# The last batch's MLP by seven quarter products in place of eight, in a fused attention and mixer kernel

## The chip, the cores and the metric

The kernel runs on one core of one Trainium2 chip. The metric is the device time of one execution in microseconds (us), the median of the runs shown. Engines are named as the profile names them: PE (matrix product), PEld (its weight load), DVE (vector), ACT (activation), POOL (GpSimd), SP (a queue that here issues DMAs).

## The reference

Block-sparse attention over 4 batches, 8 heads, 768 positions and head width 64, then a mixer: a low-rank mix over the positions, and an MLP with one hidden layer of 2048, added to its own input.

```
mask = (neighbouring blocks) | (first or last block) | (three sampled blocks per row of blocks)
attn = softmax(where(mask, q @ k.T / sqrt(64), -1e9))
x    = (attn @ v), heads side by side          # (4, 768, 512)
h    = x.transpose(0, 2, 1) @ U @ V            # rank 32, over the 768 positions
u    = x + h.transpose(0, 2, 1)
out  = u + maximum(u @ w_ch1, 0) @ w_ch2       # 512 -> 2048 -> 512
```

## The kernel before

The work is done by head pairs, i = 0 to 15, four for each batch. Scores are made transposed (keys on the partitions), ACT takes their exponentials into slots of the tile est, and for i >= 4 the DVE multiplies them by the 0/1 tile mask, 1536 columns at a time (L756, two operands in SBUF). The value product (L400) takes the masked slot as the stationary operand. The DVE divides by the row sums into xh (16 bit) and xf (32 bit), the mix is added to both (L541, L542), and a transposing DMA from SP makes uT, the MLP's input with channels on the partitions.

The MLP of a batch has two layers. In w1 (L587) a unit is one block jj of 128 hidden channels and one half c of 384 positions: 4 products of 384 columns are summed in one PSUM bank, and ACT or DVE writes the positive part to a tile tT (L599, L601). In w2 (L611) a unit is a block sc of 128 positions: 16 products of 512 columns, four at a time (words W), then the DVE adds xf (L619) into a tile of, and SP sends it out. The last block of the last batch is done by last_half (L636, L644), 256 columns and then twice 128, so that its results leave in pieces; its tiles of come from a pool of two buffers.

The order on PE, DVE, ACT and SP is written by hand: the string PLAN holds one word for each piece of work, in the order in which it is issued (U: a w1 unit, W: four w2 products, a and b: the positive part on ACT or DVE, Q: scores of a pair, e: exponentials, p: mask product, V: value product, v: division, D and d: the mix, f: finish). A digit after a capital is the PSUM bank of the eight. The instructions of each engine then run in that order, and each waits for its operands. POOL is not in that list: its order is the compiler's. It casts the loaded q, k and v to 16 bit (L137, L140), issues the loads of the weights w1t and w2t, and has nothing to do in the batch-3 MLP. The casts from pair 6 on are cut into four pieces:

```
    for h in range(2):
        for ts in (slice(0, T // 2), slice(T // 2, T)):
            last = nc.gpsimd.tensor_copy(out=dst[:, h, ts], in_=ld[:, h, ts])
```

begin(i) is called when the first score of pair i comes up in PLAN, and loads(i) asks for the q, k and v of pair i + 2.

## Time and profile before

| what | value |
|---|---|
| median of 3 runs | 285.96 us (283.65 to 286.66) |
| profiled execution, from its first to its last instruction | 281.5 us |
| PE busy | 273.6 us, 97% of the span |
| DVE busy | 194.2 us, 69% |
| ACT busy | 177.9 us, 63% |
| POOL busy | 75.6 us, 27% |
| granted PE clock, mean | 0.999 |

No other time is given for the profiled execution than its span: what lies around it, the start and end of the program, is the difference to the timed runs, 2.1 to 5.2 us. A busy PE is an engine with a matmul in flight, and matmuls overlap, so 97% says that it seldom runs dry and not that it is at its peak. Rows of groups give the busy time of the group, the mean of one instruction in ns and the idle time just before, with what ended it.

### The profile page before, as it was taken

The numbers are of one execution on the slowest core, as the hardware profiler recorded it, in microseconds if no ns is written. First come the engines' busy times: TensorE is split into PE (matmuls) and PEld (weight loads), VectorE is DVE, ScalarE is ACT, GpSimd is POOL, SyncE is SP. The second block draws the span as 40 slices with busy tenths as digits, with TensorE's granted clock in tenths as the row PEclk, the third lists the DMA queues.
The fourth block names the chain that finished last, engine by engine and source line by source line (L and its number), as shares of the span: only waits on it lengthen the run. The fifth ranks groups of instructions, "written<-read, shape, count | busy, mean of one in ns | idle before, by whom it ended". The sixth has DMA issues, their size and how long they took to land.

```text
span 281.5 us, 6704 instructions
## 1 busy us (share of the span) xinstructions
PE 273.6 (97%) x2768; PEld 159.8 (57%) x2768; DVE 194.2 (69%) x347; ACT 177.9 (63%) x206; POOL 75.6 (27%) x164
## 2 busy tenths in 40 slices
PE   7899999999999999999999999999999999999993
PEld 3577775656465654656455654656547645555552
DVE  5699988988676898788677888776677871003411
ACT  3999998888668655686867555797776303451100
POOL 5379015901768050074352050060000000000000
PEclk9999999999999999999999999999999999999999
DMA  6799997999975653646351843740001062002021
GB/s 170 236 317 270 196 245 182 178 106 266 212 178 188 191 162 98 178 115 196 87 178 40 249 106 95 204 113 7 37 37 40 17 135 77 0 0 77 0 93 57
DMA packets 49118, 37.53 MB, mean 133 GB/s; under 512 B 30464, under 2 KB 45600, under 8 KB 49088
## 3 DMA queue, kind: packets, MB, share of 16 engines
q1 hardware_dynamic: 45968, 32.61, 42.9%
q0 software_dynamic: 2688, 4.19, 10.5%
q8 instruction: 21, 0.34, 0.5%
q10 hardware_dynamic: 432, 0.31, 0.4%
q14 instruction: 9, 0.07, 0.1%
HBM read 27.67 MB, written 6.29 MB: 121 GB/s over the span
## 4 chain that ended last, share of the span: by engine, by line
PE 92%; DVE 4%; DMA 2%; issue 1%; ACT 1%; SPq 0%; DVEq 0%; ACTq 0%
PE ps L587 30%; PE ps L611 29%; PE ps L400 12%; PE ps L741 10%; PE ps L697 3%; PE ps L716 2%; PE ps L529 2%; DMA qld<-in_q_dram 1%; PE ps L656 1%; DMA out_dram<-of 1%; DVE qres L686 1%; PE ps L636 1%; PE ps L670 1%; DVE kres L279 1%; ACT est L724 1%
## 5 line engine op out<-in xcount | busy, mean ns | idle before, releaser
L750 ACT ACTIVATE est<-ps 128x1536 f16<-128x1536 f32 x72 | 100.3, 1449 | 38.7 <-PE ps L741 38.7
L587 PE MATMUL ps<-uT,w1t 128*128 128x384 f16 x512 | 94.3, 326 | 0.0
L611 PE MATMUL ps<-w2t,tT 128*128 128x512 f16 x368 | 87.1, 379 | 0.0
L756 DVE TENSOR_TENSOR est<-est,mask 128x1536 f16<-128x1536 f16 x72 | 69.6, 972 | 15.2 <-ACT est L750 15.0
L599 ACT ACTIVATE tT<-ps 128x384 f16<-128x384 f32 x90 | 43.0, 494 | 43.5 <-PE ps L587 42.3
L587 PEld LDWEIGHTS <-w1t 128*128 128x128 f16 x512 | 47.6, 98 | 36.3 <-issue 5.8
L611 PEld LDWEIGHTS <-tT 128*128 128x128 f16 x368 | 34.4, 98 | 39.7 <-issue 3.8
L400 PEld LDWEIGHTS <-est 128*128 128x128 f16 x1152 | 40.8, 97 | 7.0 <-issue 1.9
L400 PE MATMUL ps<-vt,est 128*128 128x65 f16 x1152 | 43.4, 193 | 0.0
L140 POOL CAST stqld<-qld 128x192 f16<-128x192 f32 x40 | 16.9, 464 | 83.0 <-DMA qld<-in_q_dram 59.3
L619 DVE TENSOR_TENSOR of<-xf,ps 128x512 f32<-128x512 f32 x23 | 15.7, 683 | 27.6 <-PE ps L611 25.5
L601 DVE TENSOR_SCALAR tT<-ps 128x384 f16<-128x384 f32 x38 | 21.1, 555 | 18.8 <-PE ps L587 18.0
L741 PE MATMUL ps<-qpl,kpl 64*128 64x512 f16 (+1 forms) x288 | 31.3, 325 | 0.0
L706 ACT ACTIVATE est<-ps 128x768 f16<-128x768 f32 x30 | 22.5, 813 | 0.6 <-PE ps L697 0.6
L741 PEld LDWEIGHTS <-kpl 64*128 64x128 f16 x288 | 11.8, 94 | 15.9 <-issue 10.4
L140 POOL CAST stkld<-kld 128x192 f16<-128x192 f32 x40 | 18.7, 506 | 2.6 <-DMA kld<-in_k_dram 2.6
L477 DVE TENSOR_TENSOR xh<-ps,rcp 128x384 f16<-128x384 f32 x32 | 17.8, 557 | 1.1
L477 DVE TENSOR_TENSOR xf<-ps,rcp 128x384 f32<-128x384 f32 x32 | 17.5, 547 | 0.0
L541 DVE TENSOR_TENSOR xh<-xh,ps 128x384 f16<-128x384 f16 x28 | 15.3, 548 | 1.7 <-PE ps L529 1.6
L140 POOL CAST vt<-vld 128x192 f16<-128x192 f32 x40 | 15.9, 436 | 0.3 <-DMA vld<-in_v_dram 0.3
L542 DVE TENSOR_TENSOR xf<-xf,ps 128x384 f32<-128x384 f32 x28 | 15.3, 546 | 0.0
L697 PE MATMUL ps<-qres,kres 128*128 128x384 f16 x60 | 14.0, 324 | 0.8 <-DVE kres L279 0.5
(83 smaller groups left out, 149.5 us busy)
## 6 DMA issues: line engine op xcount, KB each, us to landing
vld<-in_v_dram SPq DMA_DIRECT2D x16, 384.0 KB, 5.0
out_dram<-of SPq DMA_DIRECT2D x23, 256.0 KB, 2.1
qld<-in_q_dram SPq DMA_DIRECT2D x15, 384.0 KB, 6.8
kld<-in_k_dram SPq DMA_DIRECT2D x15, 384.0 KB, 4.5
w1t<-in_moe_w_ch_dram POOLq DMA_DIRECT2D x4, 512.0 KB, 9.2
w2t<-in_moe_w_ch_dram POOLq DMA_DIRECT2D x4, 512.0 KB, 10.4
qld<-in_q_dram SPq DMA_DIRECT2D x2, 192.0 KB
uT<-xh SPq DMA_TRANSPOSE x14, 2.8
```

Of the source, the lines that this page charges most:

```text
L140: last = nc.gpsimd.tensor_copy(out=dst[:, h, ts], in_=ld[:, h, ts])
L400: nc.tensor.matmul(pav[:, sc, :], est[:, n, sc * P : (sc + 1) * P], vts[b % 2][:, 2 * hp + h, g, 0 : D + 1], start=(g == 0 and sc == 0), s ...
L477: nc.vector.tensor_tensor(out=dst, in0=pav[:, :, 0:D], in1=rcp[:, :, None].broadcast_to([P, T, D]), op=ALU.mult,)
L587: nc.tensor.matmul(pt, w1t[:, cc, jj * P : (jj + 1) * P], bts[b].uT[cc][:, c * HS : (c + 1) * HS], start=(cc == 0), stop=(cc == NCC - 1), ...
L599: nc.scalar.activation(out=dst, in_=pt, func=AF.Relu)
L601: nc.vector.tensor_scalar_max(out=dst, in0=pt, scalar1=0.0)
L611: nc.tensor.matmul(po, tts[b, c, jj][:, s * P : (s + 1) * P], w2t[:, jj, :], start=(jj == 0), stop=(jj == NJJ - 1),)
L697: nc.tensor.matmul(ps[:, c], kT[:, h, g * P : (g + 1) * P], qT[:, h, c * HS : (c + 1) * HS], start=True, stop=True,)
L706: lambda: nc.scalar.activation(out=dst, in_=ps, func=AF.Exp, scale=0.125),
L741: nc.tensor.matmul(units[h][:, u * S + lo : u * S + hi], kT[drows[h], g * P : (g + 1) * P], qT[drows[h], lo:hi], start=True, stop=True, sk ...
L750: nc.scalar.activation(out=both[h], in_=units[h].rearrange("p (g n) -> p g n", g=2), func=AF.Exp, scale=0.125,)
L756: lambda: nc.vector.tensor_mul(out=both[h], in0=both[h], in1=mask[:, 2 * j : 2 * j + 2, :]),
```

## The change

Only the last batch's MLP changes. Each of its two products is split into halves along all three of its dimensions, and Strassen's scheme in Winograd's form takes 7 products of quarters in place of 8, each layer by itself. The sums of quarters that go in are 16-bit tiles:

- six sums of weights on POOL (weight_sum 0 to 5), called in begin(8), begin(9), begin(10) and begin(15), and two more (6 and 7) written over quarters of w1t and w2t, called at the words q.6 and q.7. Sums 0 to 2, 6 and 7 have 2048 elements on each partition; 3 to 5 are two instructions each, of 1024. The tiles qres and kres become one tile, whose space sums 0 to 2 take over;
- four sums of the input uT on the DVE (words t, 768 elements), which lie in the space of mask;
- for the second layer, four sums of hidden quarters for each of 8 blocks (words s, 384 elements), three on the DVE and one on POOL.

The products of a unit (words g for the first layer, 2 matmuls of 384 columns; words h for the second, 2 matmuls of 256) collect in three PSUM accumulators, X, Y and B. X is read three times on the way, between its products: in the first layer ACT copies it out (words c), then the DVE adds Y or B to the copy (words o), and the positive part is taken in place in SBUF by DVE, ACT or POOL (words r with 0, 1, 2). In the second layer the DVE adds each accumulator to xf (words e, 256 columns) and SP sends xf itself out. last_half goes; so do U, W, a, b and f for the last batch. The words of PLAN before q.6 are the same as before.

```diff
--- before.py
+++ after.py
@@ -118,8 +118,9 @@
     est = consts.tile([P, NEST, S], FP16, name="est")
     mask = consts.tile([P, T, S], FP16, name="mask")
     kmask = consts.tile([P, S], FP16, name="kmask")
-    qres = [consts.tile([P, 2, S], FP16, name=f"qres{i}") for i in range(2)]
-    kres = [consts.tile([P, 2, S], FP16, name=f"kres{i}") for i in range(2)]
+    res = consts.tile([P, 4, 2, S], FP16, name="res")
+    qres = [res[:, i] for i in range(2)]
+    kres = [res[:, 2 + i] for i in range(2)]
     drows = [slice(0, D), slice(D, P)]
     mrows = [slice(D, D + NB), slice(0, NB)]
     qpl = [consts.tile([P, S], FP16, name=f"qpl{i}") for i in range(2)]
@@ -411,7 +412,6 @@
 
         def __init__(self):
             self.xh = {}
-            self.uT = {}
 
         @cached_property
         def xf(self):
@@ -421,39 +421,56 @@
         def a16(self):
             return misc.tile([P, HD], FP16, tag="a16", name="a16", bufs=2)
 
+        @cached_property
+        def uT(self):
+            return upool.tile([P, NCC, S], FP16, tag="uT", name="uT")
+
         def turned(self, cc):
-            if cc not in self.uT:
-                self.uT[cc] = upool.tile([P, S], FP16, tag=f"uT{cc}", name=f"uT{cc}")
-            return self.uT[cc]
+            return self.uT[:, cc]
 
 
 
 
 
     PLAN = """
...
-    a d D6 D0 D1 d D2 d D3 d W d d U6 W a W W6 f W W W W7 f W W W U6 f U0 a U1 a U7 a U6 a U4 a
-    U7 b U1 a U4 a W6 a W U7 U0 a U1 a U2 a U7 a U3 a U0 a U7 a U1 a U5 a U7 a W a U7 W a W4 f W
-    U7 W b W U7 f U6 a U0 b U7 a W6 b U0 W b U7 U0 b W a U0 U7 b U1 b W a L4 f W2 l W W W W4 f W
-    W W L7 f l
...
+    v U6 a M0 b U7 m U2 a D6 U0 a d D5 U1 a d D7 W4 a d D6 D0 D1 d D2 d D3 d W d d U6 q.6 W a W W6 f W W
+    W W7 f W W W q.7 f g.2.1.0 t.3 g.0.1.1 t.1 c.2.1 g.0.2.2 c.0.1 g.1.1.3 t.2 g.6.1.4 c.1.1 o.0.1
+    g.1.5.5 c.6.1 g.0.6 t.4 g.2.5.6 c.0.2 g.6.2.7 g.5.1.2 o.6.1 g.0.7 c.5.1 g.1.6 c.0.3 g.2.2.7 g.5.6
+    c.1.2 o.2.1 g.2.6 c.5.2 g.1.7 c.2.2 g.0.5.7 g.5.7 c.1.3 o.0.3 g.0.4 c.5.3 g.1.4 o.1.3 o.0.4 g.0.3
+    g.1.3 r.0.0.1 o.0.2 g.5.4 g.1.2.1 o.1.2 o.1.4 g.5.5.7 o.5.4 r.0.1.0 r.1.1.2 g.4.5.3 o.1.1 g.4.1.5
...
+    h.1.4.1 e.0.3 h.1.4.2 h.1.4.3 h.0.4.0 h.0.4.1 e.1.5 h.0.4.2 h.0.4.3 h.2.4.1 h.2.4.2 e.0.5 h.2.4.3
+    h.1.5.2 h.1.5.3 e.2.5 h.0.5.0.0 h.0.5.1 e.1.4 h.0.5.2 h.0.5.3 h.1.3.0 h.1.3.1 e.0.4 h.1.3.2 h.1.3.3
+    h.0.3.0 h.0.3.1 e.1.6 h.0.3.2 h.0.3.3 e.0.6
     """
 
     class Pair:
@@ -587,7 +604,7 @@
             nc.tensor.matmul(
                 pt,
                 w1t[:, cc, jj * P : (jj + 1) * P],
-                bts[b].uT[cc][:, c * HS : (c + 1) * HS],
+                bts[b].uT[:, cc, c * HS : (c + 1) * HS],
                 start=(cc == 0), stop=(cc == NCC - 1), skip_group_check=True,
             )
         if ccs[-1] < NCC - 1:
@@ -623,33 +640,171 @@
 
             then("f", finish)
 
-    def last_half(c, n):
...
+    sw = res.rearrange("p a b s -> p (a b s)").rearrange(
+        "p (k c j) -> p k c j", k=3, c=2
+    )
+    tw = {}
+    tu = mask[:, 0:4, :].rearrange("p k (c n) -> p k c n", c=2)
+    tq = est.rearrange("p n (c s) -> p (n c) s", c=2)
+    NH, CM, DM = NJJ // 2, CH // 2, HD // 2
+
+    def minus(engine, out, in0, in1):
+        engine.tensor_tensor(out=out, in0=in0, in1=in1, op=ALU.subtract)
+
+    def weight_sum(k):
+
+        a11, a21 = w1t[:, 0:2, 0:CM], w1t[:, 0:2, CM:]
+        a12, a22 = w1t[:, 2:4, 0:CM], w1t[:, 2:4, CM:]
+        b11, b21 = w2t[:, 0:NH, 0:DM], w2t[:, NH:, 0:DM]
+        b12, b22 = w2t[:, 0:NH, DM:], w2t[:, NH:, DM:]
+        g = nc.gpsimd
+        if k == 0:
+            g.tensor_tensor(out=sw[:, 0], in0=a21, in1=a22, op=ALU.add)
+        elif k == 1:
+            minus(g, sw[:, 1], sw[:, 0], a11)
+        elif k == 2:
+            minus(g, sw[:, 2], a12, sw[:, 1])
+        elif k < 6:
+            for n in range(2):
+                js = slice(n * NH // 2, (n + 1) * NH // 2)
+                tw[k - 3, n] = ldpool.tile(
+                    [P, NH // 2, DM], FP16, tag="ld" + ("qld", "kld", "v")[k - 3],
+                    name="tw",
                 )
+                in0 = (b12, b22, b21)[k - 3][:, js]
+                in1 = b11[:, js] if k == 3 else tw[k - 4, n]
+                minus(g, tw[k - 3, n], in0, in1)
+        elif k == 6:
+            minus(g, a21, a11, a21)
+        else:
+            minus(g, b12, b22, b12)
+
+    def input_sum(k):
+        u = bts[B - 1].uT
+        b11, b12 = u[:, 0:2, 0:HS], u[:, 0:2, HS:]
+        b21, b22 = u[:, 2:4, 0:HS], u[:, 2:4, HS:]
+        in0, in1 = {
+            1: (b12, b11), 2: (b22, tu[:, 0]), 3: (b22, b12), 4: (b21, tu[:, 1])
+        }[k]
+        minus(nc.vector, tu[:, k - 1], in0, in1)
+
+    acc = {}
+
+    def product(key, pairs_, first, n=None):
+        if n is not None:
+            acc[key] = bank(n, [P, pairs_[0][1].shape[-1]], FP32)
+        for i, (lhsT, rhs) in enumerate(pairs_):
+            nc.tensor.matmul(
+                acc[key], lhsT, rhs, start=(first and i == 0),
+                stop=(i == len(pairs_) - 1), skip_group_check=True,
+            )
+
+    ACC = {1: "X", 2: "Y", 3: "B", 4: "X", 5: "B", 6: "X", 7: "X"}
+
+    def up(j, p, n=None):
+
+        u = bts[B - 1].uT
+        lo, hi = slice(j * P, (j + 1) * P), slice(CM + j * P, CM + (j + 1) * P)
+        terms = []
+        for c in range(2):
+            terms.append({
+                1: (w1t[:, c, lo], u[:, c, 0:HS]),
+                2: (w1t[:, 2 + c, lo], u[:, 2 + c, 0:HS]),
+                3: (sw[:, 2, c, lo], u[:, 2 + c, HS:]),
+                4: (w1t[:, 2 + c, hi], tu[:, 3, c]),
+                5: (sw[:, 0, c, lo], tu[:, 0, c]),
+                6: (sw[:, 1, c, lo], tu[:, 1, c]),
+                7: (w1t[:, c, hi], tu[:, 2, c]),
+            }[p])
+        product((ACC[p], j), terms, p in (1, 2, 5), n)
+
+    spare = [t_.bitcast(FP32) for t_ in (*qpl, *kpl)]
+    for vt in vts:
+        flat = vt.rearrange("p h t d -> p (h t d)").bitcast(FP32)
+        spare += [flat[:, n * HS : (n + 1) * HS] for n in range(4)]
+    turn = iter(range(NJJ * P))
+    half = {}
+
+    def up_copy(j, k):
+
+        half[j, k] = spare[next(turn) % len(spare)]
+        nc.scalar.copy(out=half[j, k], in_=acc["X", j])
+
+    def up_out(j, k):
+
+        if k == 4:
+            nc.scalar.activation(out=tq[:, 4 * j + 3], in_=acc["X", j], func=AF.Relu)
+        else:
+            nc.vector.tensor_add(
+                out=tq[:, 4 * j + {1: 0, 2: 2, 3: 1}[k]],
+                in0=half[j, k], in1=acc["Y" if k == 1 else "B", j],
+            )
+
+    def up_relu(j, k, engine):
+
+        x = tq[:, 4 * j : 4 * j + 2] if k == 0 else tq[:, 4 * j + 2]
+        if engine == 0:
+            nc.vector.tensor_scalar_max(out=x, in0=x, scalar1=0.0)
+        elif engine == 1:
+            nc.scalar.activation(out=x, in_=x, func=AF.Relu)
+        else:
+            nc.gpsimd.tensor_scalar_max(out=x, in0=x, scalar1=0.0)
+
+    ts_ = {}
+
+    def token_sum(j, k):
+
+        a11, a22, a21, a12 = (tq[:, 4 * j + n] for n in range(4))
+        if k != 3:
+            ts_[j, k] = tpool.tile([P, HS], FP16, tag="tT", name="tT")
+        if k == 1:
+            nc.vector.tensor_add(out=ts_[j, 1], in0=a21, in1=a22)
+        elif k == 2:
+            minus(nc.vector, ts_[j, 2], ts_[j, 1], a11)
+        elif k == 3:
+            minus(nc.gpsimd, a21, a11, a21)
+        else:
+            minus(nc.vector, ts_[j, 4], a12, ts_[j, 2])
+
+    NPT = 4
+
+    def weight(k, j):
+        n, j = divmod(j, NH // 2)
+        return tw[k, n][:, j]
+
+    def down(t, p, part, n=None):
+
+        s = slice(t * P, (t + 1) * P)
+        terms = []
+        for j in range(part * NH // NPT, (part + 1) * NH // NPT):
+            a = {1: 0, 2: 3, 4: 1, 7: 2}.get(p)
+            a = ts_[j, {5: 1, 6: 2, 3: 4}[p]] if a is None else tq[:, 4 * j + a]
+            if p in (4, 5, 6):
+                w = weight({4: 2, 5: 0, 6: 1}[p], j)
+            else:
+                w = {1: w2t[:, j, 0:DM], 2: w2t[:, NH + j, 0:DM],
+                     3: w2t[:, NH + j, DM:], 7: w2t[:, j, DM:]}[p]
+            terms.append((a[:, s], w))
+        product((ACC[p] + "2", t), terms, p in (1, 2, 5) and part == 0, n)
+
+    def down_out(t, k):
+
+        a, row, col = {
+            0: ("X", t, 0), 1: ("Y", t, 0), 2: ("X", t, 1), 3: ("X", 3 + t, 1),
+            4: ("B", 3 + t, 1), 5: ("X", 3 + t, 0), 6: ("B", t, 1),
+        }[k]
+        ch = slice(col * DM, (col + 1) * DM)
+        x = bts[B - 1].xf[:, row, ch]
+        nc.vector.tensor_add(out=x, in0=x, in1=acc[a + "2", t])
+        if k in (1, 4, 5, 6):
+            nc.sync.dma_start(
+                out=out[B - 1].rearrange("(p t) d -> p t d", t=T)[:, row, ch], in_=x
+            )
+
+    calls = {
+        "t": input_sum, "g": up, "c": up_copy, "o": up_out, "r": up_relu, "s": token_sum,
+        "h": down, "e": down_out, "q": weight_sum,
+    }
 
     def mask_part(g, c, n):
         pm = bank(n, [P, HS], FP32)
@@ -794,6 +949,8 @@
             loads(m)
         if i == HP:
             hold(kpl[1])
+        for k in {8: (0,), 9: (1,), 10: (2,), 15: (3, 4, 5)}.get(i, ()):
+            weight_sum(k)
 
     def first_scores():
         for i in range(HP):
@@ -844,9 +1001,8 @@
         "K": ((mask_part, g, c) for g, c in each(range(T), (0, 1))),
         "P": ((lambda n, jj=jj: w1(0, 0, jj, n, range(2)),) for jj in range(NPART)),
         "C": ((lambda jj=jj: w1(0, 0, jj, ccs=(2, 3)),) for jj in range(NPART)),
-        "U": ((w1, b, c, jj) for b, c, jj in each(range(B), (0, 1), range(NJJ))[NPART:]),
-        "W": ((w2, b, sc, part) for b, sc, part in each(range(B), range(T), range(4))),
-        "L": ((last_half, c) for c in range(2)),
+        "U": ((w1, b, c, jj) for b, c, jj in each(range(B - 1), (0, 1), range(NJJ))[NPART:]),
+        "W": ((w2, b, sc, part) for b, sc, part in each(range(B - 1), range(T), range(4))),
         "H": ((quad,) for _ in range(NPAIR * T)),
         "Q": ((two_halves,) for _ in range(NPAIR * T)),
     }
@@ -860,7 +1016,10 @@
     ):
         for word in PLAN.split():
             kind = word[0]
-            if kind.isupper():
+            if "." in word:
+                fn, *args = word.split(".")
+                calls[fn](*map(int, args))
+            elif kind.isupper():
                 fn, *args = next(steps[kind])
                 fn(*args, *map(int, word[1:]))
             elif kind in "ab":
```

## The prediction

> **What bounds the kernel now.** I read the page first: PE is busy for 97% of the span, the other engines for 69% and less. Then the windows of the last 56 us, since the change edits the last batch, then the timeline there and the groups by line.
>
> ```profile
> span 281.5 us, 6704 instructions
> ...
> PE 273.6 (97%) x2768; PEld 159.8 (57%) x2768; DVE 194.2 (69%) x347; ACT 177.9 (63%) x206; POOL 75.6 (27%) x164
> ```
>
> ```profile
> 235.50:277.10 41.60, 41.58 (x256) 23.57 (x254) 9.00 (x15) 11.76 (x24) 0.00 (x0) 1.00 0.10 37
> 277.10:281.60 4.50, 0.00 (x0) 0.00 (x0) 0.57 (x2) 0.00 (x0) 0.00 (x0) 0.96 0.22 71
> ```
>
> The columns are the stretch, its length, the busy time of PE, PEld, DVE, ACT and POOL with counts, clock, DMA share and GB/s. From 235.5 to 277.1 PE runs the batch-3 MLP without a gap while DVE works 9.0 us, ACT 11.8 us and POOL not at all: the stage lasts as long as its columns take. The last 4.5 us are the way out. Each PE product saved is time saved, as long as nothing else becomes late.
>
> ```profile
> 243.05 7.15 PE ps L587 x44
> ...
> 266.64 1.75 PE ps L636 x16
> 268.38 6.92 PE ps L611 x32
> ```
>
> These pieces of the chain that ended last price a product in a stream: 7.15/44 = 0.163 us for 384 columns, 1.75/16 = 0.109 for 256, 6.92/32 = 0.216 for 512. That of 256 has a new stationary operand for each product, as the new second layer has, so weight loads stay hidden there.
>
> The second view is POOL against the DVE, since the change gives both new work.
>
> ```profile
> L756 DVE TENSOR_TENSOR est<-est,mask x72: 941/957/1156, 46.1 to 216.3; 128x1536 f16<-128x1536 f16 x72
> L140 POOL CAST stkld<-kld x40: 339/344/1112, 51.9 to 186.1; 128x192 f16<-128x192 f32 x40
> L137 POOL CAST vt<-vld x6: 826/827/845, 8.5 to 43.1; 128x768 f16<-128x768 f32 x6
> ```
>
> The three numbers are minimum, median and maximum in ns. A cast of 0.34 us takes up to 1.11, the 0.77 more being most of one mask product, and a mask product of 0.957 takes up to 1.156, 0.2 more, part of one cast. Each waits for what is left of the other. The neighbours in time agree: it is casts beside a mask product that are long; beside DVE work with an operand in PSUM (L541, L601, L477) they keep 0.34. A DVE instruction with two SBUF operands and a POOL instruction exclude each other here.
>
> **Part by part.** The sum is made against the span of 281.5 us; the median of the runs is 4.5 above it, and I add the change of the span to the median.
>
> (a) Products. Before: 41.6 us. After: 7 x 8 units of 2 products of 384 columns, 112 x 0.163 = 18.3; and 7 x 3 x 8 = 168 of 256, 168 x 0.109 = 18.3; together 36.6. **-5.0 us** if the stream stays dense.
>
> (b) The way out. Before, the last add waits for a buffer of of until a DMA has landed:
>
> ```profile
> 278.17 0.29 DVE L644 TENSOR_TENSOR of<-xf,ps 128x128 f32<-128x128 f32 x1 [0.77 <-DMA out_dram<-of]
> 278.48 0.33 SPq L647 DMA_DIRECT2D out_dram<-of  x1
> ```
>
> From the last matmul at 277.1 to the end it is 4.4 us, from the end of that add to the end of the span 3.1. After, xf itself is sent, so that wait goes: 0.05 + 0.42 (the 256-column add of L644) + 3.1 = 3.5. **-0.9 us.** The last DMA is 128 KB where it was 64; the 256 KB issues of L620 land in 2.1 us, no later than this tail allows.
>
> (c) Start of the new MLP. q.7 is released by the last batch-2 product at 235.5. It is a POOL sum of 2048 elements with two operands. The trace has no POOL sum. The casts of L137 and L140 give (827 - 344)/576 = 0.84 ns per element and 0.18 us fixed; if the second operand is free, q.7 takes 1.9 us, if it takes its own turn 3.6. I take 3.6, since the cast reads one element for each that it writes and the sum reads two. The DVE first does the finish of batch 2 (0.69, one operand in PSUM, no conflict), at 236.2 it wants t.3, two SBUF operands, and has to wait until 235.5 + 3.6 = 239.1. t.3 and t.1 cost half of L756's row each, 0.48, so that g.1.5.5, which needs t.1, starts at 240.1. PE has five units ahead of it, 5 x 0.326, done at 237.1. **+3.0 us**, and +1.3 with 1.9 us, +0.1 if the two don't exclude each other. Behind t.3 on the DVE stand t.1, t.2 and the first o; the copies of ACT go on. The sum q.6 starts in a stretch where the DVE only has PSUM operands (L541, L542, L619), so it costs nothing; if it ran late, the p = 7 products would wait.
>
> (d) The rest of the new MLP. DVE work up to the last first-layer unit g.6.3: 4 t x 0.48, 23 o at the 0.47 from start to start of L541 and L542, 13 s at 0.3 (a quarter of L756's row and some 0.06 fixed), 6 r at 0.25 (no row has them; L601 bounds them at 0.56, nothing below): 1.9 + 10.8 + 3.9 + 1.5 = 18.1 us. PE at that point has done 56 g and 9 h, 18.3 + 2.0 = 20.3. The DVE has 2.2 us in hand, ACT (24 copies and 8 relus at 0.49, 15.7) has more. What eats this is POOL: by then 4 sums of up to 0.83 and 5 relus of 0.5 to 0.83, 7 us of work, and 19 of the DVE's instructions have only SBUF operands. If every POOL piece held the DVE up for its whole length, 18.1 + 7 - 20.3 = 4.8 us; if none does, 0.3 is left for the hand-overs of X. With POOL busy 4 tenths of the time and 0.4 us lost at a meeting, 19 x 0.4 x 0.4 = 3.0, 0.8 more than is in hand; with the hand-overs I take **+1.5 us**. Later the DVE has 84 h of 0.22 to cover 21 e of 0.42, and is early.
>
> (e) Sums 0 to 5 on POOL, in the attention of pairs 8 to 15 or before. Three of 3.6 us and six of 0.18 + 1024 x 1.68 = 1.9. POOL is idle for 73% of the span, so the casts, and SP's transposes behind them, have time. But the mask products need the DVE, and some have no slack:
>
> ```profile
> 125.76 1.90 DVE L756 TENSOR_TENSOR est<-est,mask 128x1536 f16<-128x1536 f16 x2
> 126.54 1.25 PE L400 MATMUL ps<-vt,est 128*128 128x65 f16 x36
> ```
>
> The value products begin at 126.54, before the second mask product has ended. In each pair the last two of six stand so close (0.3 to 3 us before their use), the other four have 4 us and more. POOL's order is not in the plan: at 47 to 49 us the trace runs the weight-load markers of hold (L778) ahead of casts that the code asks for first, so where the sums run cannot be read. Nothing is lost where they meet only products with slack. Where a sum of 3.6 starts just in front of a tight one, PE stands still for up to 3.0. At worst two of the long sums and two short ones do so: 7 us. Half of the long ones at half a length, 3 x 0.5 x 1.8 = 2.7, short ones inside their slack: I take **+2.6 us**.
>
> The Trainium skill has two rules against this change that the rows only touch. "SBUF — State Buffer", section "Who interferes with whom", says that the second to issue is blocked until the first has finished, whatever its length; no row here shows it for a POOL instruction of over 0.35 us. "GPSIMD Engine Reference", section "Elementwise — side-by-side cycle accounting", gives 4.5 us for a sum of 2048 elements; by it (c) would be +3.9 and the total about 1.5 us more, an estimate.
>
> (f) Matmuls stay the same elsewhere; the single tile uT, the reuse of mask, est, qres and kres and the copies into qpl, kpl and vts are free, because their last readers (L756 to 217, L697 to 42) are done long before.
>
> Sum: -5.0 - 0.9 + 3.0 + 1.5 + 2.6 = **+1.2 us**: span 282.7, median 285.96 + 1.2 = **287.2 us**. Within its own terms this case runs from 284 to 290.
>
> **The rivals.**
>
> *The arithmetic gain stands.* POOL's sums fall between the DVE's SBUF work and q.7 is short or doesn't exclude t.3: -5.9 + 0.1 + 0.5 + 0.6 = -4.7, 281.3 us. For it: POOL has been idle at both ends, and most DVE work in this MLP has a PSUM operand. Against it: q.7 and t.3 are released within 0.7 us of each other. It decides when (c) to (e) together stay under 3 us.
>
> *Attention pays.* Mask products wait for sums 0 to 5 where the value products follow at once: (e) at 7 us, +5.6, 291.6 us: slower. For it: the 1.156 and 1.112 above, and that a backlog on a DVE busy for 69 to 80% stays for several products. Against it: four of six mask products have slack. It decides once (e) passes about 4.5 us.
>
> *The first layer runs at the pace of its accumulators.* X needs four times 0.33 of product and 0.6 of copy with its hand-overs, 3.7 us a block where PE has 2.3; three banks a block let two or three blocks run at once in eight banks, and any late DVE add keeps a bank. Then (d) is 4.8: +4.5, 290.5 us. Against it: the plan puts five blocks in flight at the start.
>
> That the change leaves PE's work as it was can be excluded: 280 products with 86,016 columns stand for the 98,304 of before.
>
> **How the numbers follow.** Forecast 0.42, the gain stands 0.22, attention pays 0.21, accumulators 0.15. About 1% (2.9 us) is what a measurement of this kernel can tell from no change, as its three runs lie 3.0 us apart. Faster by over 1%: the second case and a little of the forecast's lower edge, 0.24. Slower by over 1%: nearly all of the two slow cases, 0.34, and the upper edge of the forecast, 0.05: 0.38 after rounding. Within 1%: 0.38. The range goes from 281.0, where the gain stands, to 293.0, just past the case in which attention pays.
>
> **What would show it.** Right: 112 and 168 products in the last stage at 0.163 and 0.109; a hole of some 3 us in PE about 1.6 us after the stage's start, ended by the DVE's t.1, with a POOL sum just before; single mask products of 2 to 4 us in L756's maximum; holes in PE at L400 behind them; 3.5 us from last matmul to end. Wrong: L756's maximum stays near 1.16 and the stage begins with no hole, which would be the first rival; or POOL's sums are much shorter than 1.9 or longer than 3.6.

## The result and the profile after

The changed kernel takes 298.17 us (median of 4 runs, 296.39 to 299.0), the kernel before, in the same session, 286.31 us (283.65 to 287.24). The ratio is 1.045, 95% interval 1.038 to 1.052: slower by 11.9 us, where 287.2 was forecast.

The profiled execution took 299.0 us for a span of 297.1 us; in every profiled run here the time is 1.8 to 1.9 us more than the span. The span is 15.6 us longer than that of before. The medians differ by less because the profiled execution of before was a quick one (281.5 + 1.9 = 283.4) and that of after the longest of its four.

From the page of the changed kernel:

```profile
span 297.1 us, 6881 instructions
...
PE 276.6 (93%) x2792; PEld 165.8 (56%) x2792; DVE 235.9 (79%) x412; ACT 182.0 (61%) x217; POOL 126.5 (43%) x188
...
PEclk9999999989799999999999999999999999999999
...
L911 DVE TENSOR_TENSOR est<-est,mask 128x1536 f16<-128x1536 f16 x72 | 84.0, 1174 | 12.7 <-ACT est L905 12.6
```

L911 is the mask product that was L756: 84.0 us for the same 72 instructions where it was 69.6. Its least, median and greatest length, in ns, were 941/957/1156 before and are now:

```profile
L911 DVE TENSOR_TENSOR est<-est,mask x72: 942/958/5317, 47.6 to 230.0; 128x1536 f16<-128x1536 f16 x72
```

The granted clock has a dent in slices 9 to 11, between 60 and 80 us. That is batch 1, far ahead of the last batch, which the change is about.

**Where the 15.6 us lie.** The order of the plan's words up to q.6 is the same in both kernels, so the start of each value product (L400 before, L401 after) can be compared with its like. The lag grows by 1.5 us before the first value product. The loads are not later there: the first four that the trace times land within 0.2 us of those before. But PE's products of 384 columns follow each other at 0.32 us from 8.0 to 9.9 us, where it is 0.16 in the kernel before. This start comes and goes: the lag is 0.1 us or less in seven of the twelve experiments and 1.3 to 2.8 in five. It then grows by 1.3 at pair 4, by 9.4 from there to the value products of pair 5, by 1.6 at pair 12 (sums 3 to 5 start between 178 and 207 us), and by nothing elsewhere: **12.2 us in the attention**. The last stage, from the end of the last batch-2 product to the end, takes 48.0 us where it took 46.1: **+1.9 us**.

**The attention.** POOL's timeline after:

```profile
45.30 4.05 POOL L662 TENSOR_TENSOR res<-w1t 128x2048 f16<-128x2048 f16 x1
...
57.89 4.05 POOL L652 TENSOR_TENSOR res<-res,w1t 128x2048 f16<-128x2048 f16 x1
61.89 3.05 POOL L358 DMA_DIRECT2D w2t<-in_moe_w_ch_dram  x4
64.91 1.23 POOL L141 CAST stqld<-qld 128x192 f16<-128x192 f32 x4
66.07 1.21 POOL L141 CAST stkld<-kld 128x192 f16<-128x192 f32 x4
67.26 4.05 POOL L652 TENSOR_TENSOR res<-w1t,res 128x2048 f16<-128x2048 f16 x1
71.27 2.66 POOL L141 CAST vt<-vld 128x192 f16<-128x192 f32 x4
```

Sums 0 to 2 are coded in begin(8) to begin(10), but POOL runs them at 45, 58 and 67 us, once w1t is there and whenever it has nothing else. The DVE's and PE's timelines at the same time (start, length; in brackets the idle time before and what ended it):

```profile
58.86 3.89 DVE L911 TENSOR_TENSOR est<-est,mask 128x1536 f16<-128x1536 f16 x1
62.68 0.55 DVE L618 TENSOR_SCALAR tT<-ps 128x384 f16<-128x384 f32 x1
...
66.81 6.33 DVE L911 TENSOR_TENSOR est<-est,mask 128x1536 f16<-128x1536 f16 x2
73.06 0.55 DVE L618 TENSOR_SCALAR tT<-ps 128x384 f16<-128x384 f32 x1
```

```profile
63.28 0.83 PE L896 MATMUL ps<-qpl,kpl 64*128 64x512 f16 x8 [2.77 <-DVE tT L618]
64.04 5.11 PE L604 MATMUL ps<-uT,w1t 128*128 128x384 f16 x20
...
73.66 2.91 PE L604 MATMUL ps<-uT,w1t 128*128 128x384 f16 x12 [3.33 <-DVE tT L618]
```

The product of 58.86 ends 0.8 us after the sum of 57.89 does. That of 66.81 arrives in the middle of a cast, and the casts and the whole next sum go ahead of it: 5.3 us instead of 0.94. What then holds PE is not the mask product but the positive part (L618) queued behind it on the DVE: a PSUM bank stays full and PE stands for 2.8 and 3.3 us. The two products are the first and the third of the six of pair 5, which were early in the kernel before:

```profile
56.11 0.95 DVE L756 TENSOR_TENSOR est<-est,mask 128x1536 f16<-128x1536 f16 x1
...
60.32 1.88 DVE L756 TENSOR_TENSOR est<-est,mask 128x1536 f16<-128x1536 f16 x2
```

There they end at 57.1 and 61.3 us, 7.9 and 3.8 us ahead of the value products, which begin at 65.06. That does not help, because the positive parts stand in the same queue. After each hole the clock falls (columns: length, busy PE, PEld, DVE, ACT, POOL, then clock, DMA share, GB/s):

```profile
60.00:64.00 4.00, 1.23 (x14) 0.68 (x11) 4.00 (x3) 0.71 (x2) 4.00 (x4) 1.00 0.60 170
64.00:68.00 4.00, 4.00 (x16) 1.89 (x15) 2.78 (x5) 2.79 (x2) 4.00 (x11) 0.57 1.12 185
68.00:72.00 4.00, 2.33 (x19) 1.08 (x18) 4.00 (x1) 2.94 (x4) 4.00 (x2) 1.00 1.18 189
72.00:74.80 2.80, 1.14 (x8) 0.68 (x8) 2.36 (x5) 0.72 (x1) 1.92 (x4) 1.00 1.17 194
74.80:78.20 3.40, 3.40 (x39) 2.56 (x38) 2.46 (x4) 0.49 (x1) 0.00 (x0) 0.50 1.57 176
```

From 64.6 to 68.0 and from 74.8 to 78.2 it is 0.5, and products of 384 columns follow each other at 0.32 us, not 0.16: some 1.7 us lost each time. Two holes of 6.1 us together and twice 1.7 make 9.5, the 9.4 of pair 5.

**The last stage.** Windows of the changed kernel, and a piece of its chain that ended last:

```profile
249.20:293.60 44.40, 38.68 (x280) 26.56 (x278) 36.29 (x81) 15.37 (x35) 18.56 (x14) 1.00 0.10 34
293.60:297.10 3.50, 0.02 (x1) 0.00 (x0) 0.42 (x1) 0.00 (x0) 0.00 (x0) 0.94 0.30 103
```

```profile
281.01 12.62 PE ps L697 x114
```

12.62 us for 114 products is 0.111 each. From 249.2 to 293.6 the starts of successive matmuls show 7.8 us of holes (starts over 0.08 us later than in the stream), so the products themselves take 44.4 - 7.8 = 36.6 us, and the way out 3.5. The holes begin with sum 7 (timelines of POOL, DVE and PE):

```profile
247.50 4.06 POOL L652 TENSOR_TENSOR w2t<-w2t 128x2048 f16<-128x2048 f16 x1 [3.16 <-PE ps L628]
...
249.78 2.66 DVE L652 TENSOR_TENSOR mask<-uT 128x768 f16<-128x768 f16 x2
...
252.50 1.42 PE L697 MATMUL ps<-mask,res 128*128 128x384 f16 x6 [1.73 <-DVE mask L652]
```

t.3 waits until the sum ends at 251.56, and PE for t.1 behind it: holes of 1.9 and 0.3. The other 5.6 us come later, from 260 to 281. The groups of operation and shape in this stage show POOL's part in them:

```profile
L652 POOL TENSOR_TENSOR est<-est 128x384 f16<-128x384 f16 x8 | 7.4, 936 | 1.9 <-DVE tT L761 1.9
...
L751 POOL TENSOR_SCALAR est<-est 128x768 f16<-128x768 f16 x3 | 6.4, 2136 | 2.1 <-DVE est L738 2.1
...
L761 DVE TENSOR_TENSOR tT<-est 128x384 f16<-128x384 f16 x8 | 5.2, 656 | 0.0
L652 DVE TENSOR_TENSOR tT<-tT,est 128x384 f16<-128x384 f16 x8 | 4.8, 625 | 0.0
...
L652 DVE TENSOR_TENSOR tT<-est,tT 128x384 f16<-128x384 f16 x8 | 2.5, 346 | 0.0
...
L747 DVE TENSOR_SCALAR est<-est 128x768 f16<-128x768 f16 x4 | 1.4, 349 | 0.0
...
L749 ACT ACTIVATE est<-est 128x768 f16<-128x768 f16 x1 | 0.8, 846 | 0.0
```

The positive part of 768 elements takes POOL 2.14 us, ACT 0.85 and the DVE 0.35. The DVE's own sums of 384 elements last 0.346 us undisturbed, and 0.63 to 0.66 in the two groups that meet POOL.

### The profile page after: what moved, and what is told of

Its sections match the earlier page's. It is cut to its first block, busy times and chain, and to the rows that moved or that the text cites. A ratio compares the mean times of both kernels' runs of the same rounds, so it can differ in the third digit from the quotient of the medians.

```text
span 297.1 us, 6881 instructions
## 1 busy us (share of the span) xinstructions
PE 276.6 (93%) x2792; PEld 165.8 (56%) x2792; DVE 235.9 (79%) x412; ACT 182.0 (61%) x217; POOL 126.5 (43%) x188
## 4 chain that ended last, share of the span: by engine, by line
PE 74%; DVE 14%; POOL 3%; issue 3%; DMA 2%; SPq 1%; ACT 1%; DVEq 0%; ACTq 0%
PE ps L628 20%; PE ps L604 20%; PE ps L401 11%; PE ps L896 8%; PE ps L697 6%; DVE est L911 4%; POOL est L751 3%; DMA qld<-in_q_dram 2%; PE ps L852 2%; DVE tT L652 2%; PE ps L546 2%; PE ps L871 1%; DVE tT L761 1%; DVE mask L652 1%; DVE est L738 1%
## 5 line engine op out<-in xcount | busy, mean ns | idle before, releaser
L911 DVE TENSOR_TENSOR est<-est,mask 128x1536 f16<-128x1536 f16 x72 | 84.0, 1174 | 12.7 <-ACT est L905 12.6
L604 PE MATMUL ps<-uT,w1t 128*128 128x384 f16 x384 | 74.3, 334 | 4.1 <-DVE tT L618 4.1
L628 PE MATMUL ps<-w2t,tT 128*128 128x512 f16 x288 | 68.3, 379 | 0.3 <-DVE xf L559 0.3
L604 PEld LDWEIGHTS <-w1t 128*128 128x128 f16 x384 | 35.9, 99 | 32.7 <-issue 12.0
L401 PEld LDWEIGHTS <-est 128*128 128x128 f16 x1152 | 41.7, 98 | 7.7 <-issue 2.1
L401 PE MATMUL ps<-vt,est 128*128 128x65 f16 x1152 | 44.4, 194 | 0.2 <-DVE tT L618 0.2
L616 ACT ACTIVATE tT<-ps 128x384 f16<-128x384 f32 x66 | 31.3, 495 | 21.6 <-PE ps L604 20.6
L628 PEld LDWEIGHTS <-tT 128*128 128x128 f16 x288 | 26.7, 98 | 31.5 <-issue 4.1
L896 PE MATMUL ps<-qpl,kpl 64*128 64x512 f16 (+1 forms) x288 | 31.5, 325 | 3.8 <-DVE tT L618 2.8
L618 DVE TENSOR_SCALAR tT<-ps 128x384 f16<-128x384 f32 x30 | 16.6, 554 | 8.3 <-PE ps L604 7.9
L896 PEld LDWEIGHTS <-kpl 64*128 64x128 f16 x288 | 11.8, 94 | 19.8 <-issue 14.4
L141 POOL CAST vt<-vld 128x192 f16<-128x192 f32 x40 | 18.7, 506 | 0.0
L636 DVE TENSOR_TENSOR of<-xf,ps 128x512 f32<-128x512 f32 x18 | 12.3, 682 | 7.2 <-PE ps L628 5.2
L652 POOL TENSOR_TENSOR w1t<-w1t 128x2048 f16<-128x2048 f16 x1 | 4.1, 4067 | 31.3 <-PE ps L604 31.3
```

What stands on the lines that cost most here:

```text
L401: nc.tensor.matmul(pav[:, sc, :], est[:, n, sc * P : (sc + 1) * P], vts[b % 2][:, 2 * hp + h, g, 0 : D + 1], start=(g == 0 and sc == 0), s ...
L604: nc.tensor.matmul(pt, w1t[:, cc, jj * P : (jj + 1) * P], bts[b].uT[:, cc, c * HS : (c + 1) * HS], start=(cc == 0), stop=(cc == NCC - 1), ...
L616: nc.scalar.activation(out=dst, in_=pt, func=AF.Relu)
L618: nc.vector.tensor_scalar_max(out=dst, in0=pt, scalar1=0.0)
L628: nc.tensor.matmul(po, tts[b, c, jj][:, s * P : (s + 1) * P], w2t[:, jj, :], start=(jj == 0), stop=(jj == NJJ - 1),)
L896: nc.tensor.matmul(units[h][:, u * S + lo : u * S + hi], kT[drows[h], g * P : (g + 1) * P], qT[drows[h], lo:hi], start=True, stop=True, sk ...
```

## The experiments

Theory: a DVE instruction with two operands in SBUF and a POOL instruction that reads SBUF exclude each other, and the sums on POOL make mask products so late that PE stops and loses its clock. Rivals: POOL's queue (loads and casts that the sums delay), the new last stage, and sheer length of the single sums, which could be cut. Each ratio below is to the kernel before, run in the same session.

**Sums alone, and all but the sums.** e1_sums_only is the kernel before with the tile res, the function weight_sum and its calls in begin, sums 0 to 5, their results unused:

```diff
--- before.py
+++ e1_sums_only.py
...
+        for k in {8: (0,), 9: (1,), 10: (2,), 15: (3, 4, 5)}.get(i, ()):
+            weight_sum(k)
```

> The kernel before with nothing added but the six weight sums 0 to 5 on POOL and the one tile res; the MLP is the old one and nobody reads the sums. Theory (a whole POOL sum of 4.05 us keeps a DVE instruction with two SBUF operands out, the tight mask products are late, PE stands still and its clock falls): the attention loses what it lost in the changed kernel, 12.2 us by the delay of the value products, so 286.3 + 12 = 298 us (295 to 300), mask products of over 3 us, and two stretches of 3.4 us at half clock. Rival (the loss comes with the new MLP or its plan, and the sums only ride along): 286 to 289 us.

e2_no_sums is the changed kernel without these calls; products with sums 3 to 5 read slices of w2t instead, so part of the result is left out.

```diff
--- after.py
+++ e2_no_sums.py
-        for k in {8: (0,), 9: (1,), 10: (2,), 15: (3, 4, 5)}.get(i, ()):
-            weight_sum(k)
```

> The changed kernel without the sums 0 to 5 (the products that need them read whatever lies there, so part of the MLP's result is left out). Theory: the attention is as before, and only the last stage's difference is left, 47.9 us against 46.0, so 286.3 + 1.9 = 288 us (286.5 to 289.5); L911's maximum back at 1.16 us. Rival (the one tile res, the one tile uT or the reuse of space hold the attention up): over 291 us, with the delay of 8.6 us between the value products of pairs 4 and 5 still there.

e1: 296.74 us, ratio 1.040 (1.030 to 1.049). e2: 286.87 us, ratio 1.007 (1.002 to 1.011). Their rows of the mask product (least, median, most, in ns):

```profile
L794 DVE TENSOR_TENSOR est<-est,mask x72: 941/957/5933, 46.2 to 230.2; 128x1536 f16<-128x1536 f16 x72
```

```profile
L915 DVE TENSOR_TENSOR est<-est,mask x72: 943/958/1132, 46.1 to 216.3; 128x1536 f16<-128x1536 f16 x72
```

With the sums alone a product takes up to 5.9 us, the value products lag by 13.9 us in the end, and two stretches of 6.8 us run at half clock. Without them the lag is nothing, the last stage shows the same 7.8 us of holes, and the span is 283.4, 1.9 above before. The two losses are separate, and each is reproduced without the other.

**Is it the read?** e7_memset is e1 with each sum replaced by writes of about the same length:

```diff
--- e1_sums_only.py
+++ e7_memset.py
+    def fill(out):
+        for _ in range(4):
+            nc.gpsimd.memset(out.bitcast(FP32), 0.0)
...
-            minus(g, sw[:, 1], sw[:, 0], a11)
+            fill(sw[:, 1])
```

> The kernel before with each of the sums 0 to 5 replaced by four POOL memsets of the same tile, about the same POOL time (3.8 us and 2.1 us estimated from the memset rows at the start of the trace) and no read of SBUF; the sums' values are left out and nobody reads them. Theory (the read port is what is shared): mask products stay under 1.2 us and the time is that of the kernel before, 285.5 to 287 us. Rival (POOL's time or its writes hold the rest up): 290 us or more, up to the 296.7 of the sums.

284.26 us, ratio 0.999 (0.995 to 1.003). POOL is as busy at the same place and no product takes over 1.14 us:

```profile
57.32 8.12 POOL L666 MEMSET res<- 128x1024 f32 x9
```

So neither POOL's time nor its queue is what costs. What the sums have and the fills lack is operands read from SBUF; a fill is another operation, too, but so is a cast, and the casts, which read SBUF, shut the product out in the prediction's rows. The row of the mask product here:

```profile
L798 DVE TENSOR_TENSOR est<-est,mask x72: 942/957/1142, 46.1 to 216.3; 128x1536 f16<-128x1536 f16 x72
```

The Trainium skill, "SBUF — State Buffer", section "Who interferes with whom", says that a DVE instruction with two SBUF inputs contends with a POOL instruction that reads SBUF and not with one that only writes; this run agrees.

**Is lateness enough?** e12_late is the kernel before with nothing on POOL, but DVE writes ahead of three mask products of batch 1:

```diff
--- before.py
+++ e12_late.py
+    idle = consts.tile([P, 256], FP32, name="idle")
+    late = iter([0, 9, 0, 0, 0, 0, 11, 0, 16])
...
+                    for _ in range(next(late, 0)):
+                        nc.vector.memset(idle, 0.0)
+                    nc.vector.tensor_mul(
```

> The kernel before, with nothing of the change, but with DVE writes to an unused tile put ahead of three mask products of batch 1: 9, 11 and 16 of 256 elements, 0.27 us each by the DVE's fills of 384 elements (0.378 us) and 64 (0.112 us) in the trace of before. They make the products late by 2.4, 3.0 and 4.3 us, as the sums on POOL did in the changed kernel at the same three places (the products there were 2.5 and 2.9 us too long and, with the casts, 4.4). POOL does nothing new. Theory (the attention's loss is only what late mask products bring: holes in PE, and then the half clock): the value products of pairs 5 and later run some 10.7 us behind before, as in the changed kernel up to pair 6 (1.3 + 9.4), the granted clock shows 0.5 for about 3.4 us after each of the two large holes, and the time is about 295.5 us, in 293 to 298. Rival 1 (the half clock came with POOL's sums, not with the holes): the same holes without a half clock, and some 3.4 us less, about 292. Rival 2 (POOL's own lateness, its casts and the loads and transposes behind them, made much of the loss): the value products run less than 6 us behind, 291 or less.

303.28 us, ratio 1.063 (1.053 to 1.073). The fills follow each other at 0.38 us, not 0.27, so the products are 3.4, 4.2 and 6.1 us late, 13.7 in all where the changed kernel has 9.8. PE stands for 2.4, 4.1 and 5.4 us where it stood for 0.7, 2.8 and 3.3, and the first of these holes, too, has 6.8 us at half clock behind it (51.7 to 58.5) that the changed kernel does not have. Both make the time longer than the 295.5 forecast. The rest is as the theory has it: the lag is 5.6 us at pair 4 and 19.8 after pair 5, and never changes again. The clock in the 40 slices of the page, and the stretches behind the other two holes:

```profile
PEclk9999999687789999999999999999999999999999
```


```profile
65.30:72.10 6.80, 4.82 (x19) 2.12 (x19) 4.34 (x9) 2.79 (x2) 2.18 (x8) 0.50 1.14 266
...
79.00:85.90 6.90, 5.54 (x45) 3.47 (x45) 4.53 (x7) 0.49 (x1) 2.93 (x7) 0.51 0.71 207
```

The half clock comes with the holes and without any sum on POOL. Both rivals fall.

**Can the sums be cut?** e3_cut is the changed kernel with sums 0 to 5 in pieces of 256 elements; e6_gap is e1 in such pieces, with fills meant to stand between them (they ended up elsewhere, so most pieces follow each other directly); e9_gap2 has e6's edit with the order piece, fill, piece enforced.

```diff
--- after.py
+++ e3_cut.py
+    def in_parts(op, out, in0, in1):
+        a, n = out.shape[1], out.shape[2]
+        for i in range(a):
+            for lo in range(0, n, 256):
+                s = slice(lo, min(n, lo + 256))
+                nc.gpsimd.tensor_tensor(
+                    out=out[:, i, s], in0=in0[:, i, s], in1=in1[:, i, s], op=op
+                )
...
-            minus(g, sw[:, 1], sw[:, 0], a11)
+            in_parts(ALU.subtract, sw[:, 1], sw[:, 0], a11)
```

```diff
--- e6_gap.py
+++ e9_gap2.py
+                with ExitStack() as behind:
+                    if apart:
+                        behind.enter_context(tc.issue_after(apart[-1].ins))
+                    piece = nc.gpsimd.tensor_tensor(
...
-                nc.gpsimd.memset(apart, 0.0)
+                with tc.issue_after(piece.ins):
+                    apart.append(nc.gpsimd.memset(pause, 0.0))
```

> The changed kernel with the sums 0 to 5 cut into pieces of 256 elements, 8 for each of sums 0 to 2 and 4 for each half of 3 to 5; 6 and 7 stay whole. A piece should take 0.18 + 256 x 0.00189 = 0.66 us, so POOL works longer, 5.3 us a sum for 4.05. Theory (exclusion by whole instructions): a mask product waits 0.66 us at most for one piece, no hole of 3 us, no half clock; the attention loses 1 to 4 us, so 289 to 292 us. Rival (POOL's queue: casts and the loads of w2t come late behind the sums): at least the same loss, 298 us or more.

> The kernel before with sums 0 to 5 on POOL (as in e1_sums_only) in pieces of 256 elements, and behind each piece a POOL memset of 256 words that reads nothing. In the changed kernel with pieces and no memset, a mask product waited 6.75 us, through ten ends of pieces. Theory (the port is kept over a run of POOL sums queued back to back and passes in a pause in which POOL reads nothing): no mask product over 2.5 us and 286 + 1 to 4, 287 to 290 us. Rival (it is POOL's queue as such, casts and loads behind the sums): the queue is longer still, so 297 us or more.

> The kernel before with sums 0 to 5 on POOL in pieces of 256, and now the order fixed so that each piece has a POOL memset of 256 words, which reads nothing, ahead of the next (in e6_gap the compiler put the memsets elsewhere: its trace has the pieces back to back, and the loads of w2t behind them). Theory (long sums back to back keep the DVE out; a pause hands the port over): mask products of at most 1.7 us, no half clock, 286 to 288 us. Rival (any POOL reading in the attention costs the tight mask products about as much, cut or not): 292 us or more, with waits of over 3 us.

e3: 301.23 us, ratio 1.055 (1.047 to 1.062). e6: 293.58, 1.035 (1.028 to 1.041). e9: 302.66, 1.060 (1.053 to 1.066). Cutting alone brought no gain clear of noise: e3 stands against 1.045 of the changed kernel, e6 against 1.040 of e1, and the intervals overlap. With the pauses enforced, e9 is slower than e1. DVE and POOL of e9:

```profile
61.87 7.42 DVE L811 TENSOR_TENSOR est<-est,mask 128x1536 f16<-128x1536 f16 x2
...
78.49 10.18 DVE L811 TENSOR_TENSOR est<-est,mask 128x1536 f16<-128x1536 f16 x2
```

```profile
79.14 0.66 POOL L675 TENSOR_TENSOR res<-res,w1t 128x256 f16<-128x256 f16 x1
79.74 0.30 POOL L679 MEMSET pause<- 128x256 f32 x1
80.01 0.66 POOL L675 TENSOR_TENSOR res<-w1t,res 128x256 f16<-128x256 f16 x1
...
86.75 0.30 POOL L679 MEMSET pause<- 128x256 f32 x1
87.00 3.20 POOL L141 CAST stqld<-qld 128x192 f16<-128x192 f32 x4
```

A mask product that begins at 78.49 waits through nine whole pieces and ten pauses; it takes 9.2 us and ends at 87.65, 0.85 after the ninth piece, the last before the casts of 87.00. In e3 one waits through ten ends of pieces, 6.8 us. In e6 DVE and POOL took turns at nearly every piece from 48.5 to 57.2 us (pieces of 1.25 us on average beside products of 0.95), and there was no half clock; its lag in the attention is 7.4 us, of which 2.7, at pair 6, have another cause: POOL issues the loads of w2t behind its sums, from 59.6 to 67.9 us, and the first product of the second layer waits for them. From its chain that ended last:

```profile
66.47 0.69 POOL w2t L358
67.16 14.66 DMA w2t<-in_moe_w_ch_dram
...
81.86 1.04 PE ps L612 x4
```

So the queue rival is true for that part of that kernel. What decides whether the DVE is let in at the end of a piece stays open.

**The last stage.** e4_relu_act moves the five positive parts from POOL to ACT; e8_q7 issues sum 7 behind the four t (a small POOL copy of the last t's output, ahead of the sum, holds it back).

```diff
--- after.py
+++ e4_relu_act.py
-    g.1.3 r.0.0.1 o.0.2 g.5.4 g.1.2.1 o.1.2 o.1.4 g.5.5.7 o.5.4 r.0.1.0 r.1.1.2 g.4.5.3 o.1.1 g.4.1.5
+    g.1.3 r.0.0.1 o.0.2 g.5.4 g.1.2.1 o.1.2 o.1.4 g.5.5.7 o.5.4 r.0.1.0 r.1.1.1 g.4.5.3 o.1.1 g.4.1.5
...
```

> The changed kernel with the five relus that POOL does in the new MLP (1.25 us for 384 elements, 2.14 for 768) moved to ACT at the same places of the plan; ACT has 0.52 and 0.85 for them. Theory (the DVE's sums s and PE's second-layer products wait for these relus): of the 5.6 us of holes in PE behind the first 2.2, about 3 go, 298.2 - 3 = 295 us (294 to 296.5). Rival (the first layer is paced by its accumulators, or the DVE is simply full): 297.5 to 298.5 us.

```diff
--- after.py
+++ e8_q7.py
-    W W7 f W W W q.7 f g.2.1.0 t.3 g.0.1.1 t.1 c.2.1 g.0.2.2 c.0.1 g.1.1.3 t.2 g.6.1.4 c.1.1 o.0.1
-    g.1.5.5 c.6.1 g.0.6 t.4 g.2.5.6 c.0.2 g.6.2.7 g.5.1.2 o.6.1 g.0.7 c.5.1 g.1.6 c.0.3 g.2.2.7 g.5.6
+    W W7 f W W W f g.2.1.0 t.3 g.0.1.1 t.1 c.2.1 g.0.2.2 c.0.1 g.1.1.3 t.2 g.6.1.4 c.1.1 o.0.1
+    g.1.5.5 c.6.1 g.0.6 t.4 q.7 g.2.5.6 c.0.2 g.6.2.7 g.5.1.2 o.6.1 g.0.7 c.5.1 g.1.6 c.0.3 g.2.2.7 g.5.6
```

> The changed kernel with the POOL sum 7 held back until the DVE has made its four input sums. Theory: the hole of 1.9 + 0.3 us at the first product that needs t.1 goes, 298.2 - 2 = 296 us (295 to 297); rival (the hole only moves, as sum 7 then meets the DVE's later sums): 297.5 to 298.5 us.

e4: 294.84 us, ratio 1.034 (1.027 to 1.042), holes of the stage 5.6 us instead of 7.8. e8: 296.55, 1.044 (1.038 to 1.049), holes 6.2: the first two go from 2.16 to 0.53, all others stay. Each takes its own part of the holes and no more; by its ratio alone e8 can't be told from the changed kernel's 1.045.

**The arithmetic with the sums on the DVE.** e5_dve puts all eight weight sums and the token sum on the DVE, the weight sums at chosen words of the plan, and has e4's edit:

```diff
--- after.py
+++ e5_dve.py
-        g = nc.gpsimd
+        g = nc.vector
...
-            minus(nc.gpsimd, a21, a11, a21)
+            minus(nc.vector, a21, a11, a21)
...
-        for k in {8: (0,), 9: (1,), 10: (2,), 15: (3, 4, 5)}.get(i, ()):
-            weight_sum(k)
```

> The changed kernel with POOL taken out of its sums: weight sums 0 to 7 on the DVE at fixed places of the plan where the DVE of the kernel before stood idle for about a microsecond or more (76, 113, 133, 196, 200, 230 and 234 us of its trace), the five POOL relus on ACT, the token sum 3 on the DVE. Theory (the time went into DVE and POOL shutting each other out): attention at most 1.5 us late, no long mask product, full clock, the last stage near its dense 36.7 us with 1 to 3 us of holes, 3.5 us of way out; 281.5 - 5.9 + 1 + 2 = 278.6 us of span, a median of 281 to 285 us, ratio 0.985 to 0.997. Rival (the Strassen MLP is slow by its chain of accumulators, whoever does the sums): the last stage keeps over 5 us of holes, 287 us or more.

280.85 us, **ratio 0.989 (0.983 to 0.994)**: quicker than both kernels, by 1.1% than the one before. A sum of 2048 elements takes the DVE 1.22 us where POOL takes 4.05:

```profile
L651 DVE TENSOR_TENSOR w2t<-w2t x1: 1226/1226/1226, 234.4 to 234.4; 128x2048 f16<-128x2048 f16 x1
```

The lag in the attention is 0.7 us, all at sum 0; the clock is full, no mask product takes over 1.15 us, and the last stage has 3.2 us of holes. -5.0 - 0.9 + 0.7 + 3.2 = -2.0, the span's change -1.9.

The words q.0 to q.5 stand in the plan behind words W or U, so that the sums run at 75.9, 113.9 and 133.9 us and from 196.1 to 202.1; q.6 moves some words back. Two variants: e10_dve2 has sum 0 twelve words, or two mask products, later (the expectation says five words) and three positive parts of 768 elements on the DVE; e11_s3pool has the token sum back on POOL.

```diff
--- e5_dve.py
+++ e10_dve2.py
-    p Q f W6 e e W q.0 p U2 U0 a p a V7 Q v W e e p V7 U2 v W a p Q f W7 e e W p U6 W a p Q U6 e e W b U6 p
+    p Q f W6 e e W p U2 U0 a p a V7 Q v W e e q.0 p V7 U2 v W a p Q f W7 e e W p U6 W a p Q U6 e e W b U6 p
...
```

```diff
--- e5_dve.py
+++ e11_s3pool.py
-            minus(nc.vector, a21, a11, a21)
+            minus(nc.gpsimd, a21, a11, a21)
```

> e5_dve with two changes: weight sum 0 five words later in the plan, at a mask product that had 0.98 us of idle DVE before it and slack behind it, and the three relus of 768 elements from ACT (0.85 us) to the DVE (0.35 us). Theory: the 0.74 us by which the value products of pair 6 come late in e5_dve go, and so do some of the holes of 0.55 and 0.79 us behind ACT's relus: 280.85 - 1 = 279.8 us (279.2 to 280.6). Rival (the DVE is now too full in the last stage): 281 us or more.

> e5_dve with the eight token sums 3 given back to POOL (0.94 us each there for about 0.3 on the DVE). Theory (in that stage the DVE's sums of two SBUF operands wait for them): the holes at the second layer's first products come back, of which the kernel with only the relus moved has 0.28 + 0.48 + 1.34 us: 281.9 us (281.2 to 282.8). Rival (POOL takes work off a full DVE): 280.5 us or less.

281.58 us, ratio 0.988 (0.983 to 0.993), and 281.67, ratio 0.989 (0.984 to 0.993): by the ratios neither can be told from e5. The 279.8 expected of e10 did not come, and the rival, a DVE too full, fits its time without being shown: its profiled execution took 286.38 us, 3 to 5 more than its other five, and isn't read here. e11 lies in its range, and its trace has the three holes that were expected back (0.28, 0.48 and 1.34) with 0.29, 0.48 and 1.36; the stage has 4.0 us of holes where e5 has 3.2.

## Why the prediction was wrong, point by point

- **(a), products**: -5.0 forecast, 36.6 us forecast and 36.6 measured. **(b), way out**: 3.5 forecast, 3.5 measured.
- **(c), sum 7 against t.3**: +3.0 forecast, +2.2 measured. The mechanism, the place and t.1 as what PE waits for were right. The sum takes 4.06 us, not 3.6, but starts at 247.50, 1.7 us earlier than assumed, since it overwrites only what the first half of the last unit's products reads.
- **(d), rest of the new MLP**: +1.5 taken, 4.8 as the bound, 5.6 measured. The mis-sized term is the positive part on POOL. It was priced by the cast of the same size, 0.83 us, and takes 2.14; that of 384 takes 1.25, not 0.5. e4 removes 2.2 us of holes by moving these five alone. Another 0.8 is POOL's token sum, 0.94 us where 0.83 was the top (4.0 in e11 against 3.2 in e5). Some 2.7 stay in e5 without any POOL work, beside the 0.5 at the first two holes: 1.3 behind ACT, which came with the move of the positive parts (e4 has the same two holes, the changed kernel has not), and 1.4 whose cause is not shown.
- **(e), sums 0 to 5**: +2.6 taken, 7 as the bound, 12.2 measured. **This is the step that failed**, in its path and in its price. The path: a loss was expected only where a sum meets one of the last two mask products of a pair, through the value products, and "nothing is lost where they meet only products with slack". The meetings that cost most were with the first and the third of pair 5, which had 7.9 and 3.8 us of slack; PE stopped through the positive part (L618) behind them on the DVE, at L896 and L604. Holes at L400 were the sign named; the page of the changed kernel has 0.2 us at that line, now L401. The price was missed in three ways. The place was called unreadable and then treated as chance; in fact all three long sums ran between 45 and 71 us, in pairs 4 and 5. A meeting was bounded by the length of one sum, 3.6 us; a sum takes 4.05, and a product behind a running cast waited for the casts and a whole sum, 4.4 us. And the half clock that follows a stop of PE, twice 1.7 us here, was in no term. e12 makes the same kind of loss, holes and half clock, from lateness alone.
- **The rivals**: "attention pays" had the place and the exclusion but the same path through the value products, and its 291.6 us was still 6.6 too low, having (e) at 7. "The arithmetic gain stands" came in no run with the weight sums on POOL, and e5, at 280.85, reaches its 281.3 by another way. The accumulators' pace can be a part at most: e5 has the same products, banks and copies, and 2.7 us of holes in the rest of the stage where this rival had 4.8.
- **The bounds**: "at worst two long and two short sums" was no bound but a guess, since nothing in the trace limited how many products one sum delays, or what a stopped PE does to the clock. That put the end of the range below the result.

## What to carry to other kernels

An idle engine is room only if it shares nothing with the busy one. Before giving POOL work with operands in SBUF, look in the trace for every DVE instruction with two SBUF operands that could run meanwhile, and count as lost the whole run of POOL work in front of it. Slack of that instruction is no protection if others wait behind it on the DVE with a PSUM bank full. Add the half clock that can follow a stop of PE: a stop of 1.6 us was enough in e1. An instruction whose order no plan fixes runs when its operands are ready, not where the code has it; assume the worst place.

## What the runs showed of the hardware that was not expected

- A stop of PE can cost more than its length. Holes of 2.8 and 3.3 us were each followed by 3.4 us at half clock; of 4.1 and 5.4 us (e12) by 6.8 each, and so were one of 2.4 (e12) and one of only 1.6 us (e1, 49.5 to 51.1). The Trainium skill, "TensorE: Matmul & The Clock Gate", section "HAM oscillation — how this bites in real kernels", asks for no gaps above about 3.4 us; here shorter ones were enough.
- The length alone does not decide. In e8_q7 a hole of 2.77 us before the same products as in the changed kernel (60.0 to 62.8) was followed by no half clock, nor was one of 2.15 us in e6 (69.7 to 71.9). Within each trace the changes of the granted clock lie whole multiples of 3.41 us apart. Cut into stretches at these multiples, the hole of 2.77 us in the changed kernel has 2.1 us in one stretch, and that in e8 has 1.7 in one and 1.1 in the next. Which part of a stretch must be idle was not tested by any run.
- A DVE product is not let in at the next end of a POOL instruction: it waited 8.2 us beyond its own length through nine sums of 0.66 us with fills of 0.3 us between them (e9). In other places of the same kernels it was let in at the next end. So the rule that the prediction takes from the Trainium skill, "SBUF — State Buffer", section "Who interferes with whom", that the second is blocked until the first has finished, gives no upper bound here. No run says what decides.
- POOL's sum of two 16-bit operands takes 0.91, 2.12 and 4.05 us for 384, 1024 and 2048 elements: 0.18 us and 1.89 ns per element. Its in-place maximum of 768 takes 2.14 us, 2.6 times the cast of as many.
